# The second projection of token chunk 1 as seven products of quarter matrices, with the order of five engines written out anew

## The chip, the cores and the metric

The kernel runs on one core of a Trainium2 chip. A core has five engines that run side by side and wait for one another through semaphores: TensorE (PE in the profile; its weight loads are PEld) multiplies matrices into the eight banks of PSUM, VectorE (DVE), ScalarE (ACT) and GpSimd (POOL) work element by element, and SyncE (SP) issues most of the transfers. GpSimd cannot reach PSUM, so whatever comes out of TensorE is taken out by VectorE or ScalarE. Each engine works off its own list of instructions in order: when the first one waits, all behind it wait too.

The metric is the device time of the kernel in microseconds, the median of several runs.

## What is computed

The reference is a linear attention with decay, whose output goes, token by token, through two matrices with a periodic function between them. Cut to what matters (`q`, `k`, `v` are 4 x 8 x 768 x 64; 3072 tokens of 512 after the attention; `w_in` is 512 x 2048, `w_out` 2048 x 512):

```python
for b in range(nb):                                   # blocks of a sequence, state kv_state
    intra = np.einsum('bhic,bhjc->bhij', qb, kb) * Dmask[None]
    intra = np.einsum('bhij,bhjd->bhid', intra, vb)
    inter = np.einsum('bhid,bhde->bhie', qb * lam_pow[None], kv_state)
    out[:, :, sl] = intra + inter
    kv_state = lam_block * kv_state + np.einsum('bhsd,bhse->bhde', kb * rev_pow[None], vb)

x = out.transpose(0, 2, 1, 3).reshape(B * S, H * D)
h = x @ w_in                                          # first projection
g = h + np.sin(alpha * h) ** 2 / (alpha + 1e-9)
return g @ w_out                                      # second projection
```

## The kernel before, in words

The kernel works on 24 blocks of 128 tokens (6 for each sequence) in the attention, and on six chunks of 512 tokens (four blocks each) in the projections.

**Attention of a block s.** `scale_block(s)` multiplies q and k by powers of lam (lines 462, 472, 480, 492) and casts v to bf16 (486, 495); `piece_Q`, `piece_K`, `piece_T` transpose q and k on TensorE, with a copy out of PSUM (539, 543, 571, 516), and from block 12 on a transposing DMA takes their place. `piece_G(s, t)` puts the scores of block s (`part_S`, L612), the output of block t (`part_O`, L694, L707, L716) and the state (`part_Z`, L648, L656) into one run of TensorE; VectorE masks the scores (L623), and the output and the state are copied out (L726, L666, L672). The first four blocks go by single pieces: `piece_S`, `piece_Z`, `piece_P`, `piece_I`, with the output copied out in `evict` (L739).

**First projection of a chunk.** `unit_A(c, m)` makes 128 of the 2048 features for 512 tokens: four matmuls of 128x512 (L822), a sine on ScalarE (832), its square on ScalarE or GpSimd (836, 837) and one VectorE instruction that adds it up into the tile `gT` (839). `unit_A2(c, m, half)` makes two features' groups for half of the tokens, with eight matmuls of 128x256 (L856) and halves of the later instructions (866, 870, 871, 874). All of chunk 1 goes by `unit_A2`, first half 0, then half 1, since its blocks 6 and 7 come late.

**Second projection.** For chunks 0 and 1 it is plain: `unit_B(c, s4, mq)` multiplies 128 tokens with a quarter of the features, four matmuls of 128x512 (L887); four of these fill a bank, ScalarE copies it out (L901) and stores it. From chunk `SC = 2` on it goes by seven products instead of eight: tokens and features, and rows and columns of `w_out`, are cut into halves, and `product(c, k)` calls `unit_P` (L975) with quarters or sums of quarters, each product in two units u of eight matmuls of 128x256. What it needs beside: sums of quarters of the weights, once (`weight_sums`, L930: three for the tiles `Tw` and `Ta`, two in place in `w2`, each for p = 0 and 1), sums of quarters of `gT` for each chunk (`token_sums`, L953: 16 instructions, of which 8 in place, and 4 late ones), and seven `finish` instructions of 128x512 that copy or add up the products (1012, 1015, 1021).

**Order.** The program text makes a list of 1040 operations with their dependences. The order in which each engine issues them is written out in `_Plan.ORDER`, by their numbers in that list; a pair (n, cols) in the list of PE is n idle matmuls (`spin`, L1134). An operation that may run on more than one engine (a tuple of engines) runs where its number stands. `_settle` and `emit` follow the tables and place the semaphore waits.

Of the kernel before, what the change touches and what calls it, by code (L numbers as in the profile page):

```python
# [6 lines left out]
ACTF = mybir.ActivationFunctionType  # L7
# [6 lines left out]
class _Op:  # L14


    def __init__(self, eng, emit, dur, reads, writes, dma, after, issue, lat, runs=64):
# [13 lines left out]
        self.knows = None  # L31


class _Plan:
# [17 lines left out]
        ),  # L52
        "ACT": (
# [108 lines left out]
    @staticmethod  # L162
    def _ordered(d, o):


        if d.eng != o.eng or d.dma is not None:
            return False
        return d.eng == "PE" or not (set(d.writes) & set(o.reads) or set(d.reads) & set(o.writes))

    def emit(self):  # L170
        order = self._settle()
        place = {o: i for i, o in enumerate(order)}
        for o in order:
            for d in o.deps:
                d.needed = d.needed or not self._ordered(d, o)
# [33 lines left out]
def bass_lightning_attn__then__act_snake_kernel(  # L209
# [28 lines left out]
    NP = 4  # L238
# [1007 lines left out]
```

## Time and profile before

| | |
|---|---|
| time, median of 3 runs (lowest, highest) | 211.13 us (210.77, 211.39) |
| span of the profiled execution, first to last instruction | 209.8 us |
| granted TensorE clock, mean | 1.000 |
| DMA, read and written | 27.28 MB and 6.29 MB |

For the profiled execution only its span is given, not a time of its own; the median of the runs lies 1.3 us above that span. Times in the profile are counted from the start of the span. The busy time of TensorE is modelled by the profiler; in the chain of waits and in the stretches, a unit of four 128x512 matmuls and a unit of eight 128x256 matmuls each take the time that their successor shows. In the groups of instructions, the columns are: line, engine, operation, what is written and read, partitions x elements, count, then busy time, mean ns of one, and the idle time before them with what ended it. In a table of stretches, each row gives for every engine the busy time and, in brackets, the instructions, then the granted clock, the busy share of the DMA engines and the GB/s.

### The profile page before, as it was taken

To read this page: it belongs to the slowest core of one execution; us is meant where nothing else is said; L and a number is where in the kernel's file an instruction comes from. 1 tells how busy PE (TensorE), PEld (TensorE's weight loads), DVE (VectorE), ACT (ScalarE), POOL (GpSimd) and SP (SyncE) were. 2 spreads that over 40 slices of the span, in tenths; PEclk is the share of its full clock that TensorE was granted. 3 is DMA by queue.
4 is the path that set the end of the run, shared out by engine and by line. 5 is a ranking of instruction groups with operands and counts; after the bars stand their busy time and mean duration, and the time that the engine had idled before them with its cause. 6 is when DMAs were issued, how large, how long until landed. Compare 5 with 4: busy or idle time off the path is not lost.

```text
span 209.8 us, 4867 instructions
## 1 busy us (share of the span) xinstructions
PE 203.5 (97%) x1975; PEld 134.3 (64%) x1975; DVE 160.3 (76%) x266; ACT 158.7 (76%) x294; POOL 126.9 (60%) x130
## 2 busy tenths in 40 slices
PE   7979999999999999999998999999999999999995
PEld 6847444457677776555555667766667765666894
DVE  4884557563999866868899799889698699777643
ACT  4949995968998989999997887787963889568210
POOL 7075354994469578679885392944581957378300
DMA  4999999999998999999999920190000004000514
GB/s 141 310 318 232 206 213 237 246 229 256 220 264 205 227 245 230 223 233 196 246 271 228 213 53 0 33 271 2 3 0 3 0 23 179 3 0 0 200 40 163
DMA packets 78998, 33.35 MB, mean 159 GB/s; under 512 B 55408, under 2 KB 76160, under 8 KB 78976
## 3 DMA queue, kind: packets, MB, share of 16 engines
q1 hardware_dynamic: 73744, 27.14, 56.2%
q0 software_dynamic: 3696, 3.67, 10.5%
q10 hardware_dynamic: 1536, 2.24, 3.3%
q8 instruction: 15, 0.25, 0.5%
q14 instruction: 7, 0.06, 0.1%
HBM read 27.28 MB, written 6.29 MB: 160 GB/s over the span
## 4 chain that ended last, share of the span: by engine, by line
PE 83%; DVE 6%; DMA 3%; SPq 3%; ACT 2%; issue 1%
PE bank L822 27%; PE bank L975 22%; PE bank L887 13%; PE bank L856 10%; DMA v<-in_v_dram 3%; PE bank L716 3%; SPq L315 3%; PE bank L612 3%; DVE gT L839 2%; PE bank L694 1%; DVE Sm L623 1%; PE bank L511 1%; PE bank L656 1%; DVE w L930 1%; PE bank L534 1%; PE bank L707 1%
## 5 line engine op out<-in xcount | busy, mean ns | idle before, releaser
L822 PE MATMUL bank<-xT,w 128*128 128x512 bf16 x296 | 70.5, 379 | 0.0
L839 DVE SCALAR_TENSOR_TENSOR gT<-u,rinv,bank 128x512 bf16<-128x512 bf16 x74 | 53.6, 742 | 18.2 <-ACT u L836 12.5
L832 ACT ACTIVATE t<-bank,alpha 128x512 bf16<-128x512 f32 x74 | 50.0, 684 | 21.0 <-PE bank L822 20.5
L822 PEld LDWEIGHTS bank<-xT,w 128*128 128x128 bf16 x296 | 28.3, 98 | 28.4 <-DVE gT L839 0.4
L836 ACT ACTIVATE u<-t 128x512 bf16<-128x512 bf16 x59 | 36.5, 628 | 1.3
L837 POOL TENSOR_TENSOR u<-t 128x512 bf16<-128x512 bf16 x15 | 16.0, 1066 | 34.1 <-ACT t L832 30.5
L953 POOL TENSOR_TENSOR gT<-gT 128x512 bf16<-128x512 bf16 x24 | 27.8, 1172 | 11.2 <-DVE Xs L953 6.0
L623 DVE TENSOR_TENSOR Sm<-bank,mask 128x1024 bf16<-128x1024 f32 x24 | 29.1, 1218 | 4.3 <-PE bank L648 1.8
L887 PE MATMUL bank<-w,gT 128*128 128x512 bf16 x128 | 31.4, 380 | 0.0
L874 DVE SCALAR_TENSOR_TENSOR gT<-u,rinv,bank 128x256 bf16<-128x256 bf16 x44 | 18.8, 476 | 7.8 <-ACT u L870 6.1
L472 POOL TENSOR_TENSOR qk<-q,Lq 128x512 bf16<-128x512 f32 x20 | 21.2, 1075 | 2.8 <-DMA q<-in_q_dram 2.8
L856 PE MATMUL bank<-xT,w 128*128 128x256 bf16 x176 | 22.2, 273 | 0.0
L492 POOL TENSOR_TENSOR qk<-k,Lk 128x512 bf16<-128x512 f32 x20 | 20.9, 1053 | 0.6 <-DMA k<-in_k_dram 0.6
L866 ACT ACTIVATE t<-bank,alpha 128x256 bf16<-128x256 f32 x44 | 18.9, 476 | 2.0 <-PE bank L856 1.5
L887 PEld LDWEIGHTS bank<-w,gT 128*128 128x128 bf16 x128 | 11.7, 98 | 12.2
L856 PEld LDWEIGHTS bank<-xT,w 128*128 128x128 bf16 x176 | 16.4, 98 | 3.5 <-issue 0.3
L953 POOL TENSOR_TENSOR Xs<-gT 128x512 bf16<-128x512 bf16 x13 | 16.1, 1235 | 1.5 <-DVE gT L839 1.4
L975 PE MATMUL bank<-w,gT 128*128 128x256 bf16 (+1 forms) x136 | 16.3, 266 | 0.0
L975 PE MATMUL bank<-w,Xs 128*128 128x256 bf16 (+1 forms) x136 | 16.0, 267 | 0.1
L975 PE MATMUL bank<-ws,gT 128*128 128x256 bf16 x128 | 15.8, 273 | 0.0
L975 PEld LDWEIGHTS bank<-w,gT 128*128 128x128 bf16 x136 | 12.6, 98 | 3.2
L975 PEld LDWEIGHTS bank<-w,Xs 128*128 128x128 bf16 x136 | 12.4, 98 | 2.8 <-DVE osb L1021 0.3
(101 smaller groups left out, 276.0 us busy)
## 6 DMA issues: line engine op xcount, KB each, us to landing
q<-in_q_dram SPq DMA_DIRECT2D x12, 512.0 KB, 6.2
k<-in_k_dram SPq DMA_DIRECT2D x24, 256.0 KB, 5.5
v<-in_v_dram SPq DMA_DIRECT2D x24, 256.0 KB, 5.4
out_dram<-osb SPq DMA_DIRECT2D x14, 256.0 KB, 2.5
w<-in_moe_w_out_dram POOLq DMA_DIRECT2D x4, 512.0 KB, 11.4
w<-in_moe_w_in_dram POOLq DMA_DIRECT2D x3, 512.0 KB, 9.0
ws<-in_moe_w_in_dram SPq DMA_DIRECT2D x2, 512.0 KB, 7.5
out_dram<-osb ACTq DMA_DIRECT2D x8, 128.0 KB, 4.0
```

The source lines that it names most:

```text
L472: lambda e, a=a: e.tensor_tensor(qk2[:, j:j + 2, 4 * a:4 * a + 4, :], q32[:, jq, 4 * a:4 * a + 4, :, :].rearrange("p h t d -> p t h d"), b ...
L492: lambda e: e.tensor_tensor(qk2[:, j, H:2 * H, :], block32(k32, jl), lk, ALU.mult), 1.05,
L623: op("DVE", lambda e: e.tensor_tensor(Sm[js][:, :, :], banks[:, 512 * b0:512 * b0 + 1024].rearrange("p (c i) -> p c i", i=128), bass.AP(ma ...
L822: ins = e.matmul(ps[hb][:, c0:c1], w1[:, kc, 128 * m:128 * (m + 1)], xT[x][:, kc, c0:c1], start=(kc == 0 and c0 == lo), stop=(kc == NKC - ...
L832: op("ACT", lambda e: e.activation(t16[ju][:, w], ps[hb][:, w], ACTF.Sin, scale=alpha[:, m:m + 1]), 0.69 if hi - lo == TCH else 0.475, [ba ...
L836: lambda e: (e.activation(u16[ju][:, w], t16[ju][:, w], ACTF.Square) if e is nc.scalar else e.tensor_tensor(u16[ju][:, w], t16[ju][:, w], ...
L839: op("DVE", lambda e: e.scalar_tensor_tensor(out=gT[g][:, m, w], in0=u16[ju][:, w], scalar=rinv[:, m:m + 1], in1=ps[hb][:, w], op0=ALU.mul ...
L856: ins = e.matmul(ps[hb][:, 256 * i:256 * i + 256], w1[:, kc, 128 * (m + i):128 * (m + i + 1)], xT[x][:, kc, lo:lo + 256], start=(kc == 0 a ...
L866: op("ACT", lambda e, i=i: e.activation(t16[ju][:, 256 * i:256 * i + 256], ps[hb][:, 256 * i:256 * i + 256], ACTF.Sin, scale=alpha[:, m + ...
L887: ins = e.matmul(ps[ob][:, w], gT[g][:, m, 128 * s4:128 * (s4 + 1)], w2[:, m, w], start=(m == 0), stop=(m == NM - 1),)
L953: e.tensor_tensor(dst, in0, in1, alu), 0, rd, wr))
L975: ins = e.matmul(ps[ob][:, lo + d0:lo + d1], lhs, rhs[:, d0:d1], start=first and p == 0, stop=(p == NM // 2 - 1), skip_group_check=True)
```

## The change

`SC` goes from 2 to 1, so that chunk 1 too goes by the seven products. Its 16 calls of `unit_B`, with 4 copies and 4 stores, go; 14 calls of `unit_P`, 16 + 4 token sums, 7 `finish` instructions and 4 stores come. The ten weight sums are made before chunk 1's second half instead of before chunks 2 and 3. Attention runs in chunk 2's loop take their output bank from the ring of three that `unit_A` uses, as those of later chunks did.

Many operations that had one engine may now run on two or three (`AD`, `DP`, `ADP`). Partial-partition instructions of GpSimd at the start are held apart from their neighbours by a wait (`some`, `strict`), which takes the place of the key `select`.

All five tables of `ORDER` are new. The list now has 1061 operations. How many of each kind stand on which engine:

| operations | before | after |
|---|---|---|
| token sums (L953), VectorE / GpSimd | 43 / 37 | 49 / 51 |
| scaling of q and k, VectorE / GpSimd | 7 / 41 | 16 / 32 |
| casts of v, ScalarE / GpSimd / VectorE | 20 / 4 / 0 | 10 / 10 / 4 |
| weight sums (L930), VectorE / GpSimd | 7 / 3 | 9 / 1 |
| squares, ScalarE / GpSimd | 74 / 22 | 78 / 18 |
| finish with a subtraction or addition, VectorE | 28 | 33 |
| finish by a copy, ScalarE / VectorE | 10 / 0 | 9 / 3 |
| copies of the plain projection, ScalarE / VectorE | 8 / 0 | 2 / 2 |
| all operations with their DMA issues, ACT / DVE / POOL | 306 / 266 / 126 | 289 / 297 / 131 |

The idle matmuls at the start were (42,112), (30,128), (11,128), two single ones, (8,128), and nine of 128x512 in four places up to `piece_I(3)`; they are now (23,512), (1,512) ahead of everything and (2,128) before `piece_I(3)`.

The diff, cut to its core:

```diff
         "PE": (
-            (42,112), 39, (30,128), 57, (11,128), 55, (1,128), 53, (1,128), 59, (8,128), 61, (1,512), 62,
-            (3,512), 65, 67, 69, 70, (3,512), 73, 75, 78, 80, 82, 85, (2,512), 87, 90, 91, 93, 124, 130, 140,
+            (23, 512), (1, 512), 61, 39, 62, 53, 55, 57, 59, 69, 65, 70, 67, 75, 73, 82, 78, 87, 80, 85, 90, 91,
+            (2, 128), 93, 124, 130, 140, 136, 147, 151, 155, 144, 163, 167, 159, 230, 175, 228, 171, 183, 229,
+            191, 179, 187, 232, 206, 207, 231, 233, 209, 235, 217, 234, 215, 319, 320, 221, 236, 237, 226, 241,
...
+            483, 452, 454, 489, 499, 467, 504, 506, 511, 510, 525, 500, 481, 527, 536, 535, 520, 553, 588, 606,
...
         "DVE": (
+            326, 196, 208, 182, 194, 190, 328, 327, 28, 216, 329, 331, 330, 222, 211, 212, 332, 242, 246, 213,
...
+            424, 383, 382, 335, 408, 407, 437, 436, 429, 430, 464, 465, 409, 422, 421, 410, 484, 459, 431, 458,
+            494, 493, 411, 361, 363, 433, 386, 472, 471, 505, 509, 514, 482, 503, 530, 526, 539, 521, 556, 495,
...
         "POOL": (
+            161, 165, 173, 108, 195, 189, 199, 198, 333, 267, 262, 260, 261, 353, 280, 295, 450, 351, 281, 350,
+            316, 339, 352, 449, 376, 444, 362, 443, 544, 442, 476, 377, 477, 478, 517, 384, 385, 432, 387, 434,
+            412, 488, 546, 570, 543, 485, 487, 496, 545, 642, 479, 518, 498, 596, 580, 533, 597, 532, 619, 790,
...
         "SP": (
-            0, 2, 3, 4, 5, 6, 7, 8, 9, 10, 11, 96, 97, 112, 109, 110, 111, 113, 114, 116, 115, 117, 119, 118,
+            0, 4, 5, 2, 3, 6, 7, 8, 9, 11, 10, 96, 97, 110, 109, 112, 111, 113, 114, 118, 121, 115, 116, 117,
...
-        if d.eng != o.eng or d.dma is not None:
+        if d.eng != o.eng or d.dma is not None or d is o.strict:
...
+        last = None
+        for o in order:
+            if o.eng == "POOL" and o.dma is None:
+                if last is not None and (o.some or last.some):
+                    o.strict = last
+                    o.deps.add(last)
+                last = o
...
-    SC = 2
-    QD = ((0, 0), (0, 2), (1, 0), (1, 2))
+    SC = 1
+    AD = (("ACT", 0, 0), ("DVE", 0, 0))
+    DP = (("DVE", 0, 0), ("POOL", 0, 0))
+    ADP = (("ACT", 0, 0), ("DVE", 0, 0), ("POOL", 0, 0))
...
             pieces = pieces_of(8, None, False) + pieces_of(10, 9, False)
+            if SC == 1:
+                weight_sums(True)
+                weight_sums(False)
             for i in range(8):
                 unit_A2(1, 2 * i, 1, (5, 6, 4)[(i + 2) % 3])
+                if SC == 1 and i % 2:
+                    token_sums(1, i // 2)
...
                 if c == SC:
-                    P.lead = -100
                     weight_sums(True)
-                    P.lead = 0
-                if c == SC + 1:
+                if c == SC + 1 and SC > 1:
                     weight_sums(False)
```

What the numbers of the new list that the next section uses stand for (up to 325 they are those of the old list):

| number | operation |
|---|---|
| 75, 82, 87 | `piece_Z` of blocks 0, 1, 2 on PE |
| 80, 85 / 90, 91, 93 | `piece_P(0)`, `piece_I(1)` / `piece_P(2)`, `piece_I(2)`, `piece_I(3)` on PE |
| 124 | first `unit_A2` of chunk 0 on PE |
| 47, 48, 71, 72, 76, 77, 83, 84 | on ACT: casts of v, copies of the transposed k of blocks 2 and 3, copies of the state |
| 215, 216 and 221, 222 | attention runs with the scores of blocks 4 and 5 on PE, and their masking on DVE |
| 319, 320 | last readers in chunk 0's plain projection of the first half of `w2` |
| 326 to 331 | weight sums into `Tw` and `Ta`; 332, 333 and 334, 335 those in place in `w2`, for p = 0 and 1 |
| 360 to 363, 384 to 387, 409 to 412, 431 to 434 | token sums of chunk 1 for p = 0 to 3; the last of each four is the sum into the quarter that product 2 reads |
| 466, 483 / 499, 504 / 510, 525 | units u = 0, 1 of products 3 / 4 / 2 of chunk 1 on PE |
| 609, 608, 625, 626 | the four stores of chunk 1 on SP |

More of the change, by code (lines that the diff above doesn't have):

```diff
@@ L31, in __init__ @@
         self.knows = None
+        self.some = False
+        self.strict = None
 class _Plan:
@@ L446, in _ @@
             op("ACT", lambda e: e.copy(alpha[:, :], ps[4][:, 0:NM]), 0.2, [bank(4), "warm"], ["alpha"])
-            def QE(s, a):
-                return "DVE" if (s, a) in QD else "POOL"
             def ported(o):
@@ L478, in scale_block @@
                     for a in range(2) if s % 2 == 0 else ():
[L479 to L480 removed]
+                        ported(op(DP, lambda e, a=a: e.tensor_tensor(
                             qk2[:, j:j + 2, H + 4 * a:H + 4 * a + 4, :],
@@ L483, in scale_block @@
                             bass.AP(Lp, n * H + 4 * a, [[NP * H, 128], [H, 2], [1, 4], [0, D]]), ALU.mult),
-                           dur, [("k32", jl + a), "Lp"], [("k2", j, a), ("k2", j + 1, a)]))
+                           0.68, [("k32", jl + a), "Lp"], [("k2", j, a), ("k2", j + 1, a)]))
                     for a in range(2) if s % 2 == 0 else ():
-                        ported(op("ACT" if s and not a else "POOL", lambda e, a=a: (e.copy if e is nc.scalar else e.tensor_copy)(
+                        ported(op(ADP, lambda e, a=a: (e.copy if e is nc.scalar else e.tensor_copy)(
                             v2[:, j:j + 2, 4 * a:4 * a + 4, :],
@@ L569, in piece_K @@
                 for t in range(2):
-                    op("ACT" if s else (("DVE", 0.43, 0.0), ("ACT", 0.6, 0.0)),
+                    op(AD,
                        lambda e, t=t: (e.copy if e is nc.scalar else e.tensor_copy)(qkT[:, jt + t, 4:8, :], tps[t]),
@@ L900, in unit_B @@
                 parts = [("osb", jo, i) for i in range(lo // 256, hi // 256)]
-                op("ACT", lambda e: e.copy(osb[jo][:, w], ps[ob][:, w]), 0.59, [bank(ob)], parts)
+                op(AD, lambda e: (e.copy if e is nc.scalar else e.tensor_copy)(osb[jo][:, w], ps[ob][:, w]), 0.59, [bank(ob)], parts)
                 def store(eng):
@@ L1011, in finish @@
                 if i in (1, 3):
-                    op("ACT", lambda e: e.copy(c1 if i == 1 else ny, got), 0.59 if n == 2 else 0.37, [bank(ob)], kc if i == 1 else kn)
+                    op(AD, lambda e: (e.copy if e is nc.scalar else e.tensor_copy)(c1 if i == 1 else ny, got), 0.59, [bank(ob)], kc if i == 1 else kn)
                     return
```

42 lines of the change are left out of this document (21 added, 21 removed), and 97 rows, old and new, of the table ORDER.

## The prediction

> **What bounds the kernel now.** I read the page first, then the chain of waits, then stretches of the span, then the groups of instructions by form.
>
> ```profile
> span 209.8 us, 4867 instructions
> ...
> PE 83%; DVE 6%; DMA 3%; SPq 3%; ACT 2%; issue 1%
> ```
>
> Of the chain that ends last, 83% is TensorE. The stretches (PE, PEld, DVE, ACT, POOL busy) say where that holds:
>
> ```profile
> 19.00:49.70 30.70, 30.70 (x209) 15.72 (x207) 18.72 (x28) 24.09 (x44) 18.78 (x17) 1.00 1.17 228
> 49.70:80.20 30.50, 30.50 (x383) 22.44 (x381) 24.29 (x46) 27.95 (x60) 20.07 (x20) 1.00 0.99 233
> ...
> 104.50:124.00 19.50, 18.83 (x163) 11.63 (x158) 17.43 (x24) 16.84 (x30) 13.35 (x12) 1.00 1.01 210
> ...
> 19.00:207.20 188.20, 187.50 (x1679) 121.47 (x1676) 147.44 (x242) 145.68 (x267) 116.28 (x105) 1.00 0.68 149
> ```
>
> From 19.0 to 207.2 us TensorE is idle for 0.7 us in all, and all of it lies between 104.5 and 124. So a unit taken from TensorE is worth its time, as long as nobody else becomes late. The other three have room on average (VectorE 147 of 188), but not everywhere.
>
> The chain at the start, at the places that the change touches, and unit by unit:
>
> ```profile
> 14.49 0.62 ACT v L486
> ...
> 17.29 0.62 PE bank L648 x8
> 17.91 0.57 PE bank L759 x32
> 18.48 0.68 PE bank L779 x8
> 19.16 0.87 PE bank L856 x8
> ...
> 28.63 1.73 PE bank L887 x8
> ...
> 51.46 0.22 PE bank L511 x4
> ...
> 74.68 0.33 PE bank L612 x8
> 75.01 0.34 PE bank L707 x8
> 75.35 0.34 PE bank L716 x8
> 75.82 0.97 PE bank L887 x4
> ...
> 148.33 0.87 PE bank L975 x8
> ```
>
> The first projection starts at 19.0, and ahead of it stand the last value load (cast at 14.49), the state of block 2 (L648 at 17.29), `piece_P(2)` (0.57) and two `piece_I` (0.34 each). A unit of L887 takes 0.865, a unit of L975 0.87.
>
> **The change part by part.**
>
> *TensorE's work.* 16 units of 0.865 go (13.8), 14 of 0.87 come (12.2): **-1.6**. The 0.7 idle at 104.5 to 124 stood among weight and token sums on VectorE that are moved away; I take it as recovered, **-0.7** (bounds 0 and -0.7).
>
> *The start.* In the new PE list `piece_P(0)` and `piece_I(1)` stand behind `piece_Z(2)`; before, they ran while TensorE waited for it. That puts 0.57 + 0.34 = 0.9 on the path. `piece_Z(2)` still waits for the same value loads and the same row of state copies on ScalarE, now with casts and copies of k between; I reckon with 0.2 earlier. Start: **+0.7**, so 124 begins at 19.7. Bounds: -0.3 (k first, copies shared with VectorE, all of it hidden) and +1.2 (the first cast of `w1`, now on ScalarE, ends late too). New waits between GpSimd's mask instructions lie beside the load of lam, for which everybody waits until 4 us: nothing; without that cover under 1 us.
>
> *Vector work ahead of product 2 of chunk 1.* This is what decides. Before, chunk 1's second half (about 59 to 80 us) had plain units of L887 between its `unit_A2`, which kept TensorE busy while ScalarE and VectorE were not ready. Those units are gone; product 3 alone can run there. Unit 510 needs, for p = 0 to 3, the sums 363, 387, 412, 434 into its quarter, and these stand late: 363 on VectorE, 412 on GpSimd as the 34th instruction from 333 on. So there are three arrival times.
>
> *TensorE*, from 124 up to 511: 38 first-projection units (33.0), 16 of L887 (13.8), 4 products (3.5), 16 transposing groups of 0.22 (3.5), `piece_Z(3)` (0.6), 11 attention runs. A full run takes from 74.68 to 75.82 and 0.11 in the next unit, 1.25; the 11 hold 8 scores, 8 outputs and 6 states, worth 8.9. Sum 63.3: TensorE is at 510 at 19.7 + 63.3 = **83.0**.
>
> *GpSimd.* 333 waits for 332 on VectorE, in place on the same weights; 332 stands behind 222, 211 and 212, and 222 masks the scores of run 221. TensorE gets to 221 after 24.3 (16 + 10 units, four transposes, Z(3), the scores of block 4), at 44.0; the scores are there at 44.6, and VectorE needs 1.22 + 2 x 0.69 + 0.68: 333 starts at 47.9. Before it GpSimd has nothing left to do. From the groups of instructions:
>
> ```profile
> L874 DVE SCALAR_TENSOR_TENSOR gT<-u,rinv,bank 128x256 bf16<-128x256 bf16 x44 | 18.8, 476 | 7.8 <-ACT u L870 6.1 <-POOL u L871 1.5
> L623 DVE TENSOR_TENSOR Sm<-bank,mask 128x1024 bf16<-128x1024 f32 x24 | 29.1, 1218 | 4.3 <-PE bank L648 1.8 <-PE bank L612 1.5 <-PE bank L656 1.0
> L666 DVE CAST Zd<-bank 64x256 bf16<-64x256 f32 x8 | 3.4, 419 | 0.2
> L726 DVE CAST xT<-bank 128x512 bf16<-128x512 f32 x7 | 5.1, 734 | 1.3 <-PE bank L716 1.1 <-PE bank L656 0.3
> L480 DVE TENSOR_TENSOR qk<-k,Lp 128x512 bf16<-128x512 f32 x3 | 2.0, 689 | 0.0
> L384 DVE CAST w<-ws 128x1024 bf16<-128x1024 f32 x2 | 1.5, 740 | 0.4 <-DMA ws<-in_moe_w_in_dram 0.4
> L930 DVE TENSOR_TENSOR Ta<-w 128x1024 bf16<-128x1024 bf16 x2 | 1.4, 682 | 0.0
> L930 POOL TENSOR_TENSOR ws<-w 128x1024 bf16<-128x1024 bf16 x2 | 4.3, 2128 | 0.0
> L871 POOL TENSOR_TENSOR u<-t 128x512 bf16<-128x512 bf16 x7 | 7.3, 1041 | 10.9 <-ACT t L866 10.8
> L472 POOL TENSOR_TENSOR qk<-q,Lq 128x512 bf16<-128x512 f32 x20 | 21.2, 1075 | 2.8 <-DMA q<-in_q_dram 2.8
> L492 POOL TENSOR_TENSOR qk<-k,Lk 128x512 bf16<-128x512 f32 x20 | 20.9, 1053 | 0.6 <-DMA k<-in_k_dram 0.6
> L486 POOL CAST v<-v 128x512 bf16<-128x512 f32 x3 | 1.9, 617 | 1.3 <-DMA v<-in_v_dram 1.3
> ```
>
> and, min/median/max of the sums by tile:
>
> ```profile
> L953 POOL TENSOR_TENSOR gT<-gT x24: 1148/1156/1336, 94.7 to 198.2; 128x512 bf16<-128x512 bf16 x24
> L953 DVE TENSOR_TENSOR gT<-gT x24: 409/418/1372, 98.2 to 200.2; 128x512 bf16<-128x512 bf16 x24
> ```
>
> 333 to 412 are one weight sum (2.1), 4 squares (4.2), 9 of q (9.7), 8 of k (8.4), 4 casts (2.5) and 7 token sums (8.1): 35.0. Without one gap, 412 ends at **82.9**.
>
> *VectorE*, from 332 to 363: 38 of L874 (18.1), 6 masks (7.3), 11 copies out of PSUM between 0.42 and 0.73 (6.3 at their sizes), 2 scalings (1.4), 2 weight sums (1.4), 7 token sums (2.9), and 2 casts of v, which VectorE did not do before: half of L384's 740 below, GpSimd's 617 above, 0.4 taken. Sum 38.2. Such sums come out high, because instructions in a row overlap: for the whole stretch 19.0 to 207.2 of the kernel before the same count gives 163.5 where 147.44 were busy. So x 0.90, 34.4, and 363 ends at 47.9 + 34.4 = **82.3** if VectorE never idles.
>
> So all three would have to arrive together without a gap. They won't: where a VectorE and a GpSimd instruction both read two SBUF tensors they run in turn:
>
> ```profile
> 107.05 1.16 POOL L953 TENSOR_TENSOR gT<-gT 128x512 bf16<-128x512 bf16 x1
> 107.22 1.27 DVE L953 TENSOR_TENSOR Xs<-gT 128x512 bf16<-128x512 bf16 x1
> ...
> 108.17 2.30 POOL L930 TENSOR_TENSOR w<-w 128x1024 bf16<-128x1024 bf16 x1
> ...
> 109.07 1.95 DVE L930 TENSOR_TENSOR w<-w 128x1024 bf16<-128x1024 bf16 x1
> ```
>
> A VectorE sum of 0.41 took 1.27 and ended 0.28 after GpSimd's; one of 0.68 took 1.95. Between 47.9 and 83 VectorE has 14 such instructions, 6.8 us alone (2 scalings 1.4, 2 casts 0.8, 2 weight sums 1.4, 8 token sums 3.3). Bounds of the wait at 510: 0 if none collide, and 82.9 + 6.8 - 83.0 = 6.7 if each holds GpSimd up. Between them I take the densest stretch above: VectorE was busy 17.43 of 19.50, 0.894. 34.4 / 0.894 = 38.5, so 363 ends at 86.4: **+3.4**.
>
> The Trainium skill, "SBUF — State Buffer", section "Who interferes with whom", calls the pair of ports an exclusive lock held for the whole instruction; the rows above agree. Taken to its end it makes GpSimd and VectorE share 41.8 us in that stretch, which is the upper bound, 6.7, and a rival below.
>
> *Edits without a price.* The other moves between engines lie behind TensorE's work. Chunk 1's stores go from ScalarE's queue to SP's; behind 609 and 625 stand loads for blocks 20 to 23 and their transposes, wanted 30 us later; should a `finish` be that late, S(20) would wait, under 1 us.
>
> **The sum.** 209.8 - 1.6 - 0.7 + 0.7 + 3.4 = 211.6 of span. The median stands 1.3 above the span: **212.9**.
>
> **The rivals.**
>
> *The wait does not come (faster).* If 363 and 412 are there by 83.0, the span is 209.8 - 1.6 - 0.7 + 0.7 = 208.2, **209.5**, and 208.8 or less with a start that isn't late. For it: TensorE's slack before is nil, so every unit counts; my VectorE sum fits if it is busy 98% of that stretch. Against it: in no stretch above is it over 0.894. It decides at a wait of 2.3 us, above which the gain is gone.
>
> *Break-even.* A wait of 1.0 to 2.3 gives 210.5 to 211.8.
>
> *VectorE and GpSimd strictly in turn.* Wait 6.7: span 214.9, **216.2**. Against it: half of the in-place token sums on VectorE ran in 418 ns or less, undisturbed.
>
> *TensorE cold at the start.* The idle matmuls between the pieces from 9 to 19 us are gone.
>
> ```profile
> 1.52 3.55 PE L1134 MATMUL bank<-Xs 128*128 128x112 bf16 x42 [1.52 <-DVE Xs L410]
> ...
> 5.16 1.85 PE L1134 MATMUL bank<-Xs 128*128 128x128 bf16 x30
> ```
>
> The first 42 x 112 columns took 3.55, later 30 x 128 took 1.85, at whose rate the 42 would take 2.3: a slow start costs 1.3. Again at 19.7 that is **214.2** on top of the forecast. Against it: pieces still run every one or two us. The Trainium skill, "TensorE: Matmul & The Clock Gate", section "What's actually happening", lets the clock fall after an idle window of some 3.4 us; no row here shows one after 1.5 us.
>
> **How the numbers follow.** Forecast 0.43, no wait 0.27, break-even 0.14, strictly in turn 0.08, cold 0.08. 0.3% of 211.1, about what can be told from no change, is 0.6: under 210.5 is faster, over 211.8 slower. Faster 0.29 (no wait, and a little of break-even with a good start), same 0.14, slower 0.57. The range goes from the no-wait case with half of the late start taken off, 208.9, to 215.6, a wait of 6; the forecast's own, with waits of 2.3 to 5, is 211.8 to 214.5.
>
> **What would show it.** Right: the first L856 unit at about 19.7 instead of 19.0; TensorE idle several us between 75 and 90, ended by a token sum (L953) on GpSimd or VectorE; GpSimd idle before an L930 near 48, then without gaps; 14 x 8 more matmuls of L975 and 64 fewer of L887; no idle near 104 to 124. Wrong: TensorE without a gap from 20 to the end (then 209.5), a first unit at or before 19.0, or the wait in the `unit_A2` of chunk 1 themselves, on ScalarE's sines.

## The result, and the profile after

The kernel after takes 212.95 us (median of 16 runs, 210.86 to 214.77), the kernel before 210.94 (16 runs, 210.57 to 211.82). The ratio is 1.0069, 95% interval 1.0046 to 1.0092: slower by 0.7%. (The ratio leaves out the four slowest of the 16 runs, 214.05 and above, so it lies under the ratio of the medians.) The forecast was 212.9. The runs of the kernel after are spread over 3.9 us, those of the kernel before over 1.25; and the number was met by another sum than the forecast one.

The page of the kernel after: its span, and the share of each engine in the chain that ended last.

```profile
span 211.7 us, 4834 instructions
...
PE 70%; ACT 7%; DVE 7%; DMA 6%; POOL 5%; SPq 2%; issue 2%
```

TensorE fell from 83% of that chain to 70%; other engines now stand in it too. The stretches show the first of two things (the number behind the busy times is the granted clock):

```profile
13.00:16.00 3.00, 2.12 (x61) 1.55 (x64) 3.00 (x3) 2.63 (x6) 1.81 (x3) 1.00 1.13 331
16.00:17.00 1.00, 0.72 (x21) 0.49 (x13) 0.73 (x2) 0.95 (x3) 1.00 (x2) 0.52 1.18 316
17.00:22.00 5.00, 5.00 (x89) 4.02 (x88) 2.99 (x6) 2.04 (x4) 1.10 (x3) 0.50 1.19 196
22.00:23.00 1.00, 1.00 (x7) 0.74 (x6) 0.75 (x3) 0.00 (x0) 0.00 (x0) 0.57 1.22 202
23.00:24.00 1.00, 0.95 (x10) 0.80 (x9) 0.00 (x0) 0.90 (x3) 0.00 (x0) 1.00 1.14 171
```

From 16 to 22.6 us TensorE ran at half its clock; in the kernel before it had 1.00 throughout. In the order of TensorE's work of those microseconds (start, duration, tile, count, idle time before):

```profile
15.13 0.62 PE L656 MATMUL bank<-v,qk 64*128 64x128 bf16 x8 [0.47 <-ACT Zd L674]
15.83 0.48 PE L620 MATMUL bank<-qkT 64*64 64x128 bf16 x16
16.59 1.03 PE L656 MATMUL bank<-v,qk 64*128 64x128 bf16 x8 [0.28 <-ACT Zd L674]
17.55 1.07 PE L767 MATMUL bank<-Sm,v 64*64 64x128 bf16 x32
...
19.10 1.07 PE L767 MATMUL bank<-Sm,v 64*64 64x128 bf16 x32
...
21.14 2.76 PE L864 MATMUL bank<-xT,w 128*128 128x256 bf16 x16
23.95 0.38 PE L830 MATMUL bank<-xT,w 128*128 128x512 bf16 x1
```

`piece_P` (L767) takes 1.0 instead of 0.57, the first `unit_A2` starts at 21.14 instead of 19.0, and the first two take 2.81 to the next unit instead of 1.91. `piece_Z(2)` itself stands at 16.59, 0.7 earlier than the 17.29 of before.

The second thing is what isn't there: the wait at product 2. TensorE around it, and the sums on VectorE and GpSimd:

```profile
84.62 1.04 PE L983 MATMUL bank<-Ta,gT 128*128 128x256 bf16 x8
85.72 1.67 PE L830 MATMUL bank<-xT,w 128*128 128x512 bf16 x7
87.22 1.91 PE L983 MATMUL bank<-w,gT 128*128 128x256 bf16 x16
...
92.00 1.04 PE L983 MATMUL bank<-w,gT 128*128 128x256 bf16 x8
```

```profile
86.33 0.75 DVE L961 TENSOR_TENSOR gT<-gT 128x512 bf16<-128x512 bf16 x2
```

```profile
84.97 1.15 POOL L961 TENSOR_TENSOR gT<-gT 128x512 bf16<-128x512 bf16 x1 [0.39 <-DVE Xs L961]
87.83 4.49 POOL L961 TENSOR_TENSOR gT<-gT 128x512 bf16<-128x512 bf16 x4 [1.70 <-DVE Xs L961]
```

Product 2 (510 and 525, the 16 matmuls at 87.22) comes right behind two units, with no idle time marked before it. On VectorE the two sums at 86.33 are 361 and 363; on GpSimd the four at 87.83 are 387, 434, 412 and one of the late ones, so 412, the third at some 1.11 apiece, ends at 91.2. Had product 2 read 412, as the prediction says, it couldn't have run at 87.22. It doesn't: the table ahead of the prediction is wrong there. In `token_sums` the names are a11, a21, a12, a22 in the order of tile parity and token half, so a21 is the second half of the tokens in the even features, which is what product 2 multiplies, and the sum into it is the **second** of each four: 361, 385, 410, 432. Their last, 361, ends at 86.7. The fourth ones (363, 387, 412, 434) are for product 5, the 8 matmuls at 92.00.

Cut at the first transpose of block 4's k (T), whose rows are

```profile
41.08 0.40 PE L511 MATMUL bank<-ident,qk 128*128 128x128 bf16 x4
```

```profile
42.46 0.39 PE L518 MATMUL bank<-ident,qk 128*128 128x128 bf16 x4
```

for before and after, the spans divide like this. Before, two more units of plain projection stand ahead of T than after (235 and 234, 2 x 0.865 = 1.73); the second row moves them.

| us | first unit at | from there to T | T to the end | span |
|---|---|---|---|---|
| before | 18.99 | 22.09 | 168.72 | 209.8 |
| before, same work in each part | 18.99 | 20.36 | 170.45 | 209.8 |
| after | 21.14 | 21.32 | 169.24 | 211.7 |
| difference | +2.15 | +0.96 | -1.21 | +1.9 |

So behind T, where chunk 1's products stand, the kernel after is 1.2 shorter, and up to T it loses two and a half times as much (+3.1). Each row is one execution, and the order behind T is new as a whole: that the 1.2 comes from the products alone is not shown.

What ties the loss to the clock without any experiment is the list of the 16 runs of the kernel after by their mean granted clock:

```
clock 0.999 to 1.000   210.86 211.05 211.59
clock 0.991 to 0.992   212.06 212.18 212.43 212.74 212.82 213.08 213.32 214.67
clock 0.982 to 0.984   213.46 213.81 214.05 214.05 214.77
```

0.008 of 210 us is 1.7 us of clock lost, 3.4 us at half speed; twice that is the 6.6 us of the profiled run. The three runs with a full clock are about as fast as the kernel before.

### The profile page after: what moved, and what is told of

Its sections match the earlier page's. It is cut to its first block, busy times and chain, and to the rows that moved or that the text cites. A ratio compares the mean times of both kernels' runs of the same rounds, so it can differ in the third digit from the quotient of the medians.

```text
span 211.7 us, 4834 instructions
## 1 busy us (share of the span) xinstructions
PE 202.7 (96%) x1925; PEld 136.4 (64%) x1947; DVE 169.8 (80%) x297; ACT 154.2 (73%) x281; POOL 127.3 (60%) x135
## 4 chain that ended last, share of the span: by engine, by line
PE 70%; ACT 7%; DVE 7%; DMA 6%; POOL 5%; SPq 2%; issue 2%
PE bank L983 24%; PE bank L830 20%; PE bank L864 8%; PE bank L895 6%; POOL gT L961 4%; DMA v<-in_v_dram 3%; ACT t L840 3%; PE bank L724 2%; DMA out_dram<-osb 2%; PE bank L620 2%; SPq L325 2%; DVE gT L882 2%; DVE gT L847 2%; ACT u L844 2%; PE bank L656 1%
## 5 line engine op out<-in xcount | busy, mean ns | idle before, releaser
L961 POOL TENSOR_TENSOR gT<-gT 128x512 bf16<-128x512 bf16 x31 | 35.7, 1171 | 11.1 <-DVE Xs L961 10.3
L961 POOL TENSOR_TENSOR Xs<-gT 128x512 bf16<-128x512 bf16 x20 | 23.1, 1168 | 9.2 <-DVE gT L847 9.2
L983 PE MATMUL bank<-w,gT 128*128 128x256 bf16 (+1 forms) x168 | 20.1, 268 | 0.0
L983 PE MATMUL bank<-ws,gT 128*128 128x256 bf16 x160 | 19.9, 273 | 0.0
L983 PE MATMUL bank<-w,Xs 128*128 128x256 bf16 (+1 forms) x168 | 19.5, 268 | 0.2 <-DVE osb L1029 0.2
L983 PEld LDWEIGHTS bank<-w,gT 128*128 128x128 bf16 x168 | 15.7, 98 | 3.7
L983 PEld LDWEIGHTS bank<-ws,gT 128*128 128x128 bf16 x160 | 15.4, 98 | 3.8 <-DVE osb L1029 0.4
L499 POOL TENSOR_TENSOR qk<-k,Lk 128x512 bf16<-128x512 f32 x16 | 17.4, 1102 | 0.0
L480 POOL TENSOR_TENSOR qk<-q,Lq 128x512 bf16<-128x512 f32 x16 | 17.2, 1082 | 0.0
L895 PE MATMUL bank<-w,gT 128*128 128x512 bf16 x59 | 15.0, 379 | 0.4 <-issue 0.2
```

What stands on the lines that cost most here:

```text
L499: lambda e: e.tensor_tensor(qk2[:, j, H:2 * H, :], block32(k32, jl), lk, ALU.mult), 1.05,
L895: ins = e.matmul(ps[ob][:, w], gT[g][:, m, 128 * s4:128 * (s4 + 1)], w2[:, m, w], start=(m == 0), stop=(m == NM - 1),)
L961: e.tensor_tensor(dst, in0, in1, alu), 0, rd, wr))
L983: ins = e.matmul(ps[ob][:, lo + d0:lo + d1], lhs, rhs[:, d0:d1], start=first and p == 0, stop=(p == NM // 2 - 1), skip_group_check=True)
```

## The experiments

Three theories were weighed from here on. *Cold*: the half clock at the start makes the loss. *Order*: `piece_P(0)` and `piece_I(1)` behind `piece_Z(2)` make it (the +0.7 of the prediction). *Wait*: it is lost ahead of product 2, in whatever form (the +3.4). Line numbers in the rows of some variants are one higher than in the kernel after. The numbers are medians; each ratio is to runs of the kernel before on the same chip.

**Idle matmuls put back in the kernel after.**

```diff
-            (23, 512), (1, 512), 61, 39, 62, 53, 55, 57, 59, 69, 65, 70, 67, 75, 73, 82, 78, 87, 80, 85, 90, 91,
+            (23, 512), (1, 512), 61, 39, 62, 53, 55, 57, 59, (2, 512), 69, 65, 70, (1, 512), 67, (1, 512), 75, 73,
+            (2, 512), 82, 78, (1, 512), 87, 80, 85, 90, 91,
```

> The kernel after with seven idle matmuls of 512 columns put between the pieces of the start, where its TensorE record shows gaps of 0.18 to 0.47 us (two before the second piece of K of block 2, one before the scores of block 1, one before piece_Z(0), two before piece_Z(1), one before piece_Z(2)). Theory 'cold': the granted clock of 0.50 to 0.57 from 16 to 22.6 us is what makes the kernel after slower. Then the clock is 1.00 in every run, the two piece_P take 0.57 instead of 1.00, the first unit_A2 starts at 19.4 or earlier instead of 21.1, the span is 209.2 (+-0.3) and the time 210.9, with runs within 1 us of each other instead of 3.9. Theory 'order': the late start comes from piece_P(0) and piece_I(1) standing behind piece_Z(2); then the first unit still starts after 20 and the time stays at 212.9. Theory 'wait' (the prediction's): the time was lost ahead of product 2 of chunk 1; then it stays at 212.9 as well, wherever the start is.

Measured: 212.02 (211.04 to 212.66), ratio 1.0036 (1.0017 to 1.0056). The clock is 0.998 to 1.000 in each of 11 runs, and the spread falls from 3.9 to 1.6 us. But the gain is 0.9, not 2: the first unit still starts late.

```profile
1.93 7.92 PE L1142 MATMUL bank<-Xs 128*128 128x512 bf16 x24 [1.93 <-DVE Xs L420]
9.68 0.39 PE L568 MATMUL bank<-ident,qk 128*128 128x128 bf16 x4
...
17.41 0.62 PE L656 MATMUL bank<-v,qk 64*128 64x128 bf16 x8
17.96 0.64 PE L767 MATMUL bank<-Sm,v 64*64 64x128 bf16 x32
...
18.86 0.64 PE L767 MATMUL bank<-Sm,v 64*64 64x128 bf16 x32
...
20.08 0.34 PE L787 MATMUL bank<-qkT,Zd 128*128 128x128 bf16 x3 [0.41 <-issue]
...
20.59 2.02 PE L864 MATMUL bank<-xT,w 128*128 128x256 bf16 x16
```

This is TensorE's order of that run. The piece takes 0.6 again, so that part of *cold* holds. In this execution the block of 24 idle matmuls ended only at 9.7 and the first piece stood behind it; `piece_Z(2)` came at 17.41, and 3.2 us pass from there to the first unit. Of these, 0.9 are the two pieces that *order* names (17.96 to 18.86), and 0.4 is idle time in the last piece, which the profile puts down to no other engine (issue).

**The kernel before without its last eight idle matmuls.**

```diff
-            (3,512), 65, 67, 69, 70, (3,512), 73, 75, 78, 80, 82, 85, (2,512), 87, 90, 91, 93, 124, 130, 140,
+            65, 67, 69, 70, 73, 75, 78, 80, 82, 85, 87, 90, 91, 93, 124, 130, 140,
```

> The kernel before without its last eight idle matmuls (three before the scores of block 0, three before those of block 2, two before piece_Z(2)). Theory 'cold': TensorE then has gaps like those of the kernel after, the granted clock falls to about half somewhere between 13 and 23 us, the first unit_A2 starts 1 us or more later than 19.0, and the time is 212 to 214 with runs that differ by their clock. Theories 'order' and 'wait': those matmuls stand in time that TensorE waits anyway; clock 1.00, first unit at 19.0 or 0.2 earlier, time 210.9 (+-0.3).

Measured: 213.62 (213.46 to 213.86), ratio 1.0126 (1.0110 to 1.0143), clock 0.984 in all four runs.

```profile
13.00:14.00 1.00, 0.42 (x16) 0.27 (x16) 1.00 (x2) 0.36 (x1) 0.29 (x1) 1.00 1.13 319
14.00:15.00 1.00, 0.62 (x12) 0.50 (x16) 0.76 (x1) 0.42 (x1) 1.00 (x2) 0.92 1.10 344
15.00:16.00 1.00, 1.00 (x41) 1.00 (x44) 0.36 (x1) 0.83 (x3) 1.00 (x3) 0.50 1.10 347
16.00:21.00 5.00, 4.69 (x80) 3.69 (x69) 1.66 (x2) 3.06 (x7) 2.81 (x4) 0.50 1.25 227
```

In these stretches the clock is half from 15 us on, and the first unit starts at 21.05. Eight matmuls that compute nothing are worth 2.5 us to the kernel before. *Cold* is shown in both directions: put them in and the clock is full, take them out and it is half.

How busy TensorE is from 13 to 16 us does not decide it by itself. These are the stretches of the kernel before, with its idle matmuls:

```profile
9.00:13.00 4.00, 3.83 (x68) 2.29 (x68) 3.54 (x7) 2.38 (x6) 1.60 (x2) 1.00 1.20 294
13.00:16.00 3.00, 1.97 (x75) 1.55 (x76) 2.46 (x3) 1.77 (x5) 2.39 (x4) 1.00 1.11 338
```

From 13 to 16 it is less busy (1.97) than the kernel after (2.12), with one idle time of 0.90, and keeps its clock. From 9 to 13 it is busy 3.83 of 4 us, the kernel after 3.35, and the kernel before without the eight 2.49. The margin is thin: in three runs beside these experiments the kernel before, too, had a clock of 0.984, and took 213.6 to 214.2.

**`piece_P(0)` and `piece_I(1)` ahead of `piece_Z(2)` again**, without and with the idle matmuls:

```diff
-            (23, 512), (1, 512), 61, 39, 62, 53, 55, 57, 59, 69, 65, 70, 67, 75, 73, 82, 78, 87, 80, 85, 90, 91,
+            (23, 512), (1, 512), 61, 39, 62, 53, 55, 57, 59, 69, 65, 70, 67, 75, 73, 82, 78, 80, 85, 87, 90, 91,
```

> The kernel after with piece_P(0) and piece_I(1) ahead of piece_Z(2), as in the kernel before; no idle matmuls are added. Theory 'order': the 0.9 us that they cost behind piece_Z(2) come back whatever the clock does; first unit at 20.2, time 212.0. Theory 'cold': the gaps from 11 to 16 us stay, the clock falls to half again, and the time is 212 to 213.5 with runs that differ by their clock; if it does not fall, because piece_P(0) fills the gap before piece_Z(2), the time is 210.5 to 211.

> Both at once: the seven idle matmuls, and piece_P(0) and piece_I(1) ahead of piece_Z(2). Theory 'cold' alone: as with the idle matmuls alone, 210.9, since at full clock the two pieces take 0.8 us of which the sine and square work behind the first units gives back part; with 'order' on top of it 0.8 less, 210.1. First unit at 18.4 to 18.8 if both hold. Theory 'wait': 212.9.

Measured without idle matmuls: 211.74 (210.99 to 214.76), ratio 1.0025 (1.0007 to 1.0043); clock full in 8 of 11 runs. The first unit of the profiled run is at 20.15, as *order* said. But the clock is full in this execution too: ahead of `piece_Z(2)` the two pieces are also work in the gap in which the clock would fall. One edit changes what both theories name, and this run does not tell them apart; the 0.9 itself is read from the rows of the run with the idle matmuls put back. With the idle matmuls too: 211.69 (210.65 to 212.60), ratio 1.0026 (1.0009 to 1.0043), where 210.1 to 210.9 was expected. The first unit comes at 19.77 (18.4 to 18.8 was expected), and 1.4 us more goes at 32:

```profile
31.74 1.03 PE L830 MATMUL bank<-xT,w 128*128 128x512 bf16 x4
34.20 1.02 PE L830 MATMUL bank<-xT,w 128*128 128x512 bf16 x4 [1.44 <-DMA w<-in_moe_w_in_dram]
```

In the new list of GpSimd the load of the last quarter of `w_in` (104) stands behind a square (133). In the chain of this run that square goes from 23.22 to 24.21 and the load, issued then, lands at 34.07.

**The start of the kernel before in the kernel after**, alone, with its chunk 0 too, and two trials on top of that. The operations up to 123 take the order and the engines of before in all five tables; these are the lines that matter below:

```diff
-            (23, 512), (1, 512), 61, 39, 62, 53, 55, 57, 59, 69, 65, 70, 67, 75, 73, 82, 78, 87, 80, 85, 90, 91,
+            (42, 112), 39, (30, 128), 57, (11, 128), 55, (1, 128), 53, (1, 128), 59, (8, 128), 61, (1, 512), 62,
...
-            0, 4, 5, 2, 3, 6, 7, 8, 9, 11, 10, 96, 97, 110, 109, 112, 111, 113, 114, 118, 121, 115, 116, 117,
+            0, 2, 3, 4, 5, 6, 7, 8, 9, 10, 11, 96, 97, 112, 109, 110, 111, 113, 114, 116, 115, 117, 119, 118,
```

> The kernel after, with the start of the kernel before on all five engines (every operation up to 123: loads, masks, scalings, casts, pieces, and the idle matmuls), from the first unit_A2 on unchanged. Theory 'start': after the clock is held, what is left of the loss (0.6 to 0.9 us in the three runs with a full clock) is a first unit at 19.8 to 20.6 instead of 19.0. Then the first unit is at 19.0, the clock 1.00, and the time 210.2 to 210.8. If the first projection of chunk 0 is bound by its sines, squares and sums on ScalarE, VectorE and GpSimd and not by its start (the theory 'vector work of chunk 0'), the earlier start is lost again before T of block 4 (41.5 in the runs with idle matmuls, whatever their start), and the time stays at 211.7.

> On top of that, the first projection of chunk 0 in the order of the kernel before, on PE, ACT, DVE and POOL (operations 124 to 209; five squares go from GpSimd back to ScalarE). Theory 'vector work of chunk 0': T of block 4 then comes 1 us earlier than with the start alone. From T of block 4 to the end the kernel after took 166.1 to 166.6 in all four traces; with two units of plain projection more or less ahead of it, the whole is 19.0 + 20.4 + 166.3 = 205.7 to the last unit, a span of 208.2 and a time of 209.9, about 1.1 below the kernel before: the -1.6 of the seven products less 0.4 of small waits. Theory 'the gain is not there' (the small waits grow by what the start gives): 210.9 or more.

> The kernel of the run before, with the first unit of product 5 of chunk 1 (535) ahead of product 2 (510, 525) on PE. In the trace of the kernel after product 2 started at 87.2 without a wait; the token sums that it reads are the second of each four (361, 385, 410, 432), the last of them done at 86.7 on VectorE; the fourth ones (363, 387, 412, 434), which the prediction took for them, are read by product 5, and the last of those ended at 91.2 on GpSimd, 0.8 before product 5 started at 92.0. If that is so, product 5 ahead of product 2 makes TensorE wait 3 to 4 us there, ended by a token sum on GpSimd, and the time is 3 us (2 to 4) above the run before. If the sums are not what product 5 waits for, the exchange costs less than 0.5.

> The same kernel as two runs before, with two stores of chunk 0 (243, 239) issued on ScalarE ahead of the sines of chunk 2 (behind 248) instead of 20 to 30 operations later. In the kernel after a subtraction into that tile at 109.2 waited for a store of 104.0 to 109.1, and TensorE for it 0.24 us. Theory 'stores': 0.2 to 0.6 less than without it. Rival: the vector work behind is as late as the store, nothing (+-0.2).

Measured: 219.84, 225.67, 232.51 and 227.1: all four missed by far, for one reason, a mistake of the edit. The first unit was where it should be (19.00 in the first), but (chain of the second, then its TensorE):

```profile
24.11 0.37 SPq L326
...
24.52 13.14 DMA k<-in_k_dram
...
37.69 0.69 DVE qk L500
```

```profile
28.39 1.03 PE L896 MATMUL bank<-w,gT 128*128 128x512 bf16 x4
39.10 1.89 PE L896 MATMUL bank<-w,gT 128*128 128x512 bf16 x4 [9.68 <-DVE gT L848]
```

In the order of before, the load of k of block 4 (110) stands on SP behind one (109) that waits for a quarter of `w_in` until 24.1. Before, that did no harm, as GpSimd scaled this k late. After, VectorE scales it early, in front of the sums of chunk 0, and all wait: until 33.2 in the first run, until 37.5 to 37.8 in the others. Of the last three only one thing can be read: in the third, product 5, put ahead of product 2, made TensorE wait 3.85 us for a sum on GpSimd. The trial with the stores says nothing.

**Product 5 ahead of product 2, on a sound start** (that with idle matmuls and early `piece_P(0)`, 211.69):

```diff
-            483, 452, 454, 489, 499, 467, 504, 506, 511, 510, 525, 500, 481, 527, 536, 535, 520, 553, 588, 606,
+            483, 452, 454, 489, 499, 467, 504, 506, 511, 535, 510, 525, 500, 481, 527, 536, 520, 553, 588, 606,
```

> The kernel with idle matmuls and early piece_P(0) (211.7), with the first unit of product 5 of chunk 1 (535) ahead of product 2 (510, 525) on PE; this time on a kernel whose start is sound. In the trace of the kernel after, product 2 started at 87.2 without a wait; of each four token sums it reads the second (361, 385, 410, 432), done at 86.7; product 5 reads the fourth (363, 387, 412, 434), of which the last ended at 92.3 on GpSimd at the latest. If that reading is right, product 5 put ahead of product 2 makes TensorE wait 3 to 4 us between 86 and 91, ended by a sum on GpSimd, and the time is 214.5 (213.7 to 215.5). If these sums aren't what product 5 waits for, the exchange costs less than 0.5: 211.7 to 212.2.

Measured: 219.65 (217.61 to 220.84), ratio 1.0375 (1.0329 to 1.0421). TensorE's order and the stretches:

```profile
85.65 1.89 PE L830 MATMUL bank<-xT,w 128*128 128x512 bf16 x8
91.53 5.30 PE L983 MATMUL bank<-w,gT 128*128 128x256 bf16 x24 [3.99 <-POOL gT L961]
```

```profile
88.00:91.50 3.50, 0.00 (x0) 0.00 (x0) 2.73 (x6) 1.65 (x3) 3.39 (x4) 0.77 0.98 196
91.50:95.00 3.50, 3.47 (x17) 2.48 (x18) 0.00 (x0) 0.00 (x0) 3.50 (x4) 0.50 1.03 273
95.00:97.00 2.00, 2.00 (x11) 1.37 (x10) 0.00 (x0) 0.00 (x0) 2.00 (x3) 0.57 0.91 204
```

The wait is there, 3.99 as expected, ended by the sum 412 on GpSimd: it is product 5 that reads it. The price is higher than expected, 8.0 by the medians instead of 2.8: the wait lets the clock fall to half, three units take 5.3 us instead of 2.6, and VectorE and ScalarE, with nothing to do from 91.5 to 97, start late behind them.

**A shorter idle block, and the load of `w_in` ahead of the square.** On top of the idle matmuls and the early `piece_P(0)`, the block before the first piece is 20 long instead of 24; the second edit moves 104.

```diff
-            (23, 512), (1, 512), 61, 39, 62, 53, 55, 57, 59, 69, 65, 70, 67, 75, 73, 82, 78, 87, 80, 85, 90, 91,
+            (19, 512), (1, 512), 61, 39, 62, 53, 55, (2, 512), 57, 59, (2, 512), 69, 65, 70, (1, 512), 67, (1, 512),
+            75, 73, (1, 512), 82, 78, 80, 85, 87, 90, 91,
...
-            102, 103, 105, 27, 133, 104, 142,
+            102, 103, 105, 27, 104, 133, 142,
```

> The kernel after with piece_P(0) and piece_I(1) early and with idle matmuls between the pieces, as in the run with both, and two more edits: the block of idle matmuls ahead of everything is 20 instead of 24 long (it took 6.9 to 8.3 us in the four traces and ended at 8.6 to 10.1, after the data of the first piece of K, which VectorE had scaled at 7.5), and GpSimd issues the load of the last quarter of w_in (104) ahead of its first square (133) instead of behind it, where it waited for the first units and landed at 34.1, the unit that needs it waiting 1.44 us. Theory 'load': the start pays only when this load does not wait for it; first unit at 18.8 to 19.3, no wait on a load of w_in at 30 to 34, T of block 4 at 39.3 to 39.8, and from there 169.0 to the end of the span as in the other traces: span 208.3 to 208.8, time 210.3 (+-0.4), under the kernel before. Rival 'vector work of chunk 0': GpSimd's squares hold the units at 32 to 34 (0.34 us in the traces) by more the earlier they come: 211 or more.

> The same without the move of the load. Theory 'load': the first unit comes as early, but the load is issued only behind the first square, at about 23, and lands at 33 to 34 as before; T of block 4 at 41 or later, time 211.2 to 211.7, as with idle matmuls and early P0 alone. Rival: the load doesn't decide, and the time is that of the run before within 0.2.

Measured: both edits 211.18 (210.88 to 212.32), ratio 1.0019 (1.0000 to 1.0037); the block alone 211.84 (210.83 to 213.29), 1.0041 (1.0019 to 1.0063). Expected were 210.3 and 211.2 to 211.7, so both came out later. The load's move goes the expected way, but the intervals overlap, and the profiled run without the move had its load in time. The first is the best variant of the kernel after, 1.8 us faster than it, and not faster than the kernel before.

The profiled execution of the first (212.32) is the slowest of its twelve. The shorter block ended at 7.8 there, the first piece waited for VectorE until 9.73 with nothing in between, and the clock was half from 12 to 15 us.

```profile
9.73 0.40 PE L568 MATMUL bank<-ident,qk 128*128 128x128 bf16 x4 [1.93 <-DVE ident L425]
```

```profile
12.00:15.00 3.00, 3.00 (x35) 2.08 (x33) 1.75 (x5) 1.95 (x4) 0.20 (x1) 0.50 1.13 304
```

Its first unit came at 21.23, where 18.8 to 19.3 was expected. In the other eleven executions the mean clock is 0.998 to 1.000.

**The start of before, second try**: as in the first, but with SP's loads from the second round on as in the kernel after, and 104 ahead of 133.

```diff
-            0, 4, 5, 2, 3, 6, 7, 8, 9, 11, 10, 96, 97, 110, 109, 112,
+            0, 2, 3, 4, 5, 6, 7, 8, 9, 10, 11, 96, 97, 110, 109, 112,
```

> The kernel after with the start of the kernel before (operations up to 123 on PE with its idle matmuls, ACT, DVE and GpSimd, and the first loads on SP), but with the loads from the second round on (110, 109, 112 and so on) in the order of the kernel after, since its VectorE wants k of block 4 early: in the first try they stood in the order of the kernel before, 110 behind 109, and VectorE waited for that k until 37.7. The load of the last quarter of w_in (104) goes ahead of GpSimd's first square, as in the run with block and load. Theory 'start': from the first unit on, the hot variants of the kernel after took 20.5 to T of block 4 and 168.8 to 169.2 from there; with a first unit at 19.0 (+-0.3) that is a span of 208.5 and a time of 210.2 (209.8 to 210.7), 0.6 below the kernel before, clock 1.00. Theory 'the gain is not there': 210.8 or more with the first unit at 19.0, because the units wait in chunk 0 for sums, squares or loads that are late by themselves.

Measured: 211.73 (210.84 to 213.47), ratio 1.0017 (0.9982 to 1.0051), clock full in all runs; expected were 209.8 to 210.7. The start did what it should, the first unit at 19.15 and T at 39.78. Behind it TensorE waits twice in the profiled run:

```profile
68.22 1.05 PE L865 MATMUL bank<-xT,w 128*128 128x256 bf16 x8 [0.73 <-DVE gT L883]
...
109.33 1.92 PE L984 MATMUL bank<-w,Xs 128*128 128x256 bf16 x16 [1.46 <-DVE osb L1030]
```

```profile
108.58 0.69 DVE L1030 TENSOR_TENSOR osb<-bank,kept 128x512 f32<-128x512 f32 x1 [2.15 <-DMA out_dram<-osb]
```

The second is a `finish` of chunk 1 that may not write its output tile before a store of chunk 0 has read it; the new order issues that store on ScalarE only at 102.2, and it landed at 108.6. In the kernel after the same `finish` waited 0.94 on VectorE, and TensorE 0.24. The execution shown took 213.0, 1.3 above the variant's median, so the two waits say why this execution was late, not why the median missed the forecast.

The parts of the profiled runs side by side:

| us | first unit at | to T | T to the end | span | time (median of the variant) |
|---|---|---|---|---|---|
| before, same work in each part | 18.99 | 20.36 | 170.45 | 209.8 | not given (210.94) |
| after | 21.14 | 21.32 | 169.24 | 211.7 | 213.46 (212.95) |
| idle matmuls put back | 20.59 | 21.01 | 169.30 | 210.9 | 212.66 (212.02) |
| early P(0) | 20.15 | 20.47 | 168.88 | 209.5 | 211.29 (211.74) |
| both | 19.77 | 21.78 | 168.95 | 210.5 | 212.24 (211.69) |
| block and load | 21.23 | 20.54 | 168.83 | 210.6 | 212.32 (211.18) |
| block only | 19.66 | 20.47 | 168.97 | 209.1 | 210.83 (211.84) |
| start of before, second try | 19.15 | 20.63 | 171.22 | 211.0 | 213.0 (211.73) |

Each row is one execution, up to 1.3 from its variant's median, so the rows compare parts, not variants. Behind T, all but the last are 1.2 to 1.6 under the kernel before; with its two waits (2.2) taken off, the last is too (169.0).

## Why the number was right and the sum was not

*The products, -1.6: right as a count.* 64 matmuls of 128x512 went and 112 of 128x256 came. Behind T, 1.2 to 1.6 us are saved in the kernel after and five of its variants. With what each of them recovers of the 0.7 below, it should have been 0.4 to 0.9 more; where that went is not shown. The trace of the kernel before is of an execution some 0.5 above its median, so the saving against a typical execution may also be smaller.

*The 0.7 of idle time at 104.5 to 124: not recovered in the kernel after.* TensorE is busy 18.82 of 19.50 there, as before, now with small waits for the `finish` behind a store and for GpSimd's sums. Five variants recover most of it (19.24 to 19.43); the last does not (17.96, with its wait of 1.46).

*The start, +0.7: the mechanism was right, its size was not, and a rival came on top of it.* Of the +3.1 up to T, 0.9 is the two pieces, and 0.7 of that is taken back by the earlier `piece_Z(2)`, where the prediction reckoned with 0.2. The rest, 2.9, is the rival that the prediction gave 0.08 and priced at 1.3: TensorE cold at the start. Two counts agree with that remainder. From `piece_Z(2)` to the first unit the kernel after takes 4.55 instead of 2.6 (1.70 before, and 0.9), and the first two units lose 0.9: 2.85. And the median of its runs with the lowest clock is 214.05, with a full clock 211.05: 3.0. The step that failed there is "pieces still run every one or two us". Pieces at that pace did not hold the clock: the longest idle time in TensorE's record from 9 to 16 us is 0.47, and the clock fell. The Trainium skill, "TensorE: Matmul & The Clock Gate", section "What's actually happening", on which the prediction leaned, names an idle window of some 3.4 us. The Trainium skill, the same page, section "A second HAM failure mode: psum-queue depth-cycling", tells of a kernel whose short idle spells between groups of matmuls made the clock swing. The trace here agrees with the second.

*The wait at product 2, +3.4: wrong.* Two steps failed. First, which sum: the second of each four, not the fourth, so that GpSimd's 412 (82.9 or later in the prediction, 91.2 in the trace) has nothing to do with it; the run with product 5 first shows what it would have cost. Second, the two arrival times that remain.

From 51.34, when 333 started (47.9 in the prediction; the 8.26 idle before it came as said), VectorE needed 35.4 to the end of 361 at 86.7 and not 38.5: from 49 to 87 it was busy 0.94 of the time (10.10, 8.90, 10.00 and 6.84 in four stretches of 38.0), not the 0.894 that was taken from another stretch. The turns with GpSimd cost little: the five token sums on VectorE ahead of 361 took 0.41 to 0.58, against 0.41 alone. GpSimd's own 35.0 became 39.9, because it did wait (2.56, 0.36, 0.39 and 1.70) where the prediction let it run without a gap.

TensorE needed 66.1 from its first unit to product 2, not 63.3: 0.9 for the two units at half clock, and 1.9 because many units are followed 0.1 to 0.3 later than the 0.87 that was reckoned. In the block-only run, with a full clock, it is 65.2, and there the 38 first-projection units take 34.7 instead of 33.0. The profile marks only 0.8 and 0.4 us of these two stretches as idle, so what holds the units back is not shown; VectorE as the slower pace all along is the likely cause. At product 2 itself, 0.5 was left.

*From span to time, +1.3: too small.* In every run of these two kernels the time is 1.7 to 1.8 above the span (213.46 and 211.7, 210.86 and 209.1), so the profiled run of before, 209.8, stood for some 211.5, not for the median. That is another 0.45.

That the number was met is luck. In the span, +2.4 too little up to T (3.1 where 0.7 stood) met 2.3 too much behind it (-1.2 where -1.6 - 0.7 + 3.4 = +1.1 stood). From span to time, 0.45 too little met a profiled execution that lies 0.5 above the median. And the median itself is one of the runs that were cold for about half as long as the profiled one; runs with a full clock came at 211, those with the lowest at 214.

*What stays open.* Why no variant beat the kernel before, although most are shorter behind T. The starts of different executions differ by as much as the gain (first units at 19.66 and 21.23 with the same order on TensorE), and the one variant with an early start lost 2.2 in its profiled execution to a late store and a late sum behind it. No run kept the new order and undid the products alone. Whether the stores of chunk 0, issued earlier, would free the gain was not tried on a sound start.

## What to carry to other kernels

Idle matmuls between short pieces are part of the kernel: before taking them out, look at what else keeps TensorE dense in each stretch of a few us, and read the granted clock run by run, since one mean over the span hides it. A load, a store and the instruction that needs it belong to one order: moving an instruction to an engine that gets to it earlier moves the need for its load too, and a load behind a compute instruction in a queue is as late as that. When a sum forecasts a wait at one instruction, check in the code which operand it reads, and allow for an engine near its limit to show as many small delays instead of one wait.

## What the runs showed of the hardware

Short idle times are enough for TensorE's clock to fall: none over 0.47 us stands from 9 to 16 us of the kernel after, and the clock is half from 16 us on. How much work holds it is not settled. Of the 7 us from 9 to 16, TensorE was busy 5.47 there and 4.53 in the kernel before without its eight idle matmuls, both cold; it was busy 5.59 to 6.77 in six traces whose clock stayed full, one of them with an idle time of 1.14. The two nearest values are too close to give a limit, and with the early `piece_P(0)` the same order was full in 8 runs and cold in 3.

A wait of 3.99 us in the middle of the kernel costs another 2.7 of slow units behind it. The mean clock of 0.77 from 88 to 91.5 us there means 1.6 us at half, so it fell at about 89.9, 2.3 us after TensorE's last matmul before the wait (87.5).

The same 24 idle matmuls at the start took 6.9 to 8.3 us in four executions, and the first piece, which stands behind them, came at 8.6 to 10.1. The column of the granted clock does not show it: in the kernel after it reads 1.00 all through the block, although its first 13 matmuls take 4.7 us and the other 11 only 2.5. The Trainium skill, "TensorE: Matmul & The Clock Gate", section "What's actually happening", says that the number of slow matmuls at the start differs from run to run. The four executions agree.

A store on ScalarE's queue took 5.1 us to land in the kernel after and 6.4 in the last variant, and the `finish` that waits for it follows.
